# Linear attention and an ELU MLP on one core: token layout, row-tiled kv and TensorE transposes for the first batch

## Chip, cores and metric

The kernel runs on one core of a Trainium2 chip. The metric is the device time of one execution in microseconds (us); the median of several runs is given. PE is TensorE, ACT is ScalarE, DVE is VectorE, POOL is GpSimd; SP is the queue that issues DMA transposes and stores.

## What is computed

```python
def phi(x):                                   # 64 -> 128 -> 256 features
    proj = np.einsum('bhsd,df->bhsf', x, w_phi)
    proj = proj - np.max(np.abs(proj), axis=-1, keepdims=True)
    return np.concatenate([np.exp(proj), np.exp(-proj)], axis=-1)
q_p, k_p = (phi(q), phi(k))
kv = np.einsum('bhsf,bhsd->bhfd', k_p, v)
z = np.sum(k_p, axis=2)
num = np.einsum('bhsf,bhfd->bhsd', q_p, kv)
den = np.einsum('bhsf,bhf->bhs', q_p, z)[..., None] + 1e-06
attn = num / den
x = attn.transpose(0, 2, 1, 3).reshape(B * S, H * D)     # 4608 x 512
h = x @ w_in                                             # 4608 x 2048
g = np.where(h > 0.0, h, np.exp(np.minimum(h, 0.0)) - 1.0)
return g @ w_out                                         # 4608 x 512
```

There are 8 batches, 8 heads, 576 tokens, a head dimension of 64 and 128 features. All inputs and the output are float32; matmuls run in bfloat16.

## The kernel before

**Work and tiles.** Attention works on groups of four heads (a group is half a batch, 16 groups n = 0 to 15). 576 tokens are 4 x 128 + 64, so each head is loaded in two pieces: `kf`, `qf`, `vf` hold 512 tokens, four after one another in each of 128 partitions, and `km`, `qm`, `vm` hold the last 64 tokens of two heads, stacked in the two partition halves (`load_full`, `load_mixed`). The loads are issued by POOL and convert to bfloat16; a batch is nine DMAs.

**Attention.** `transposes(n)` has SP transpose k and q of a group by DMA, four DMAs. `stage_k` projects k (pieces c = 0, 1, 2; each is six matmuls of 64 rows by 128 columns, alternating between the upper and the lower half of the array: row-tiled work), takes the row maximum of the absolute value on DVE (`mk`), two exponentials on ACT (`EK`), and after the third piece the exponentials of the maxima (`em`). POOL then scales v by `em` into `vs` (line 273, all four heads at once) and the remainder into `vsm` (lines 284 and 290, two halves). `stage_qmax` does the same for q's maxima (`mq`), which are brought into rows by a DMA transpose of `mhl` into `mT`. `stage_q` projects q the other way round and subtracts the maxima by a second matmul with `sel`, then two exponentials give `Eq`. `stage_kv` multiplies `EK` with `vs` and `vsm` (40 matmuls of 128 rows by 65 columns per group; column 65 is the sum z). `stage_pn` multiplies `Eq` with `kv_sb`, divides on DVE (`xp`), and two DMA transposes put the result into `xT_sb`.

**The MLP** (named moe in the code) works on 9 chunks of 512 tokens. `moe_mm1` is four matmuls of 512 columns into `ph`, then exp on ACT into `e_sb` (line 168), min and max on POOL (line 169), and the choice on DVE into `gT` (line 172). `moe_mm2` is 16 matmuls of 512 columns into `po` for each 128 tokens, a copy on ACT and the store. A chunk is 32 items, 16 of the first kind and then 16 of the second.

**What sets the order.** The loop over n writes the pieces of a group in a list and puts MLP items from `pending` between them, 16 per group. A chunk goes into `pending` when its tokens are done, LAG pieces later. The Tile framework then orders each engine's instructions ahead of the run by its own estimate of when each is ready, and each engine runs its own queue strictly in that order. So POOL's queue holds load issues, v scaling and the MLP's e_sb in one row.

**Buffers.** PSUM is split in two pools: `pjp` with two buffers of two banks (projections, `pq`, `pn`) and `mpp` with four of one bank (`ph`, `po`, `kv`).

Of the kernel before, what the change touches and what calls it, by code (L numbers as in the profile page):

```python
# [7 lines left out]

# [8 lines left out]
def kernel(  # L17
# [20 lines left out]
    assert S == 4 * P + D and H == 8 and B % 2 == 0  # L38
# [5 lines left out]
    GH = 4  # L44
    NG = B * H // GH
    NI = 1 + GH * 2
    FULL = 4 * P
# [3 lines left out]
    N_CHUNK = NTOK // CHUNK  # L51

# [4 lines left out]
    small = ctx.enter_context(tc.tile_pool(name="small", bufs=3))  # L57
# [7 lines left out]
    w2 = consts.tile([P, F], BF16)  # L65
    for par in range(2):
        nc.gpsimd.dma_start(out=w2[par * D:(par + 1) * D, :], in_=w_phi)

    natural = {}

    def load_full(name, src, b, h0, h1):
        if (name, b) not in natural:
            natural[name, b] = (
                io.tile([P, H, 4 * D], BF16, name=name + "f"),
                io.tile([P, H // 2, D], BF16, name=name + "m"),
            )
        nc.gpsimd.dma_start(
            out=natural[name, b][0][:, h0:h1, :],
            in_=src[b, h0:h1, 0:FULL, :].rearrange("h (p s) d -> p h (s d)", s=4),
        )  # L80

    def load_mixed(name, src, b):
        pairs = src[b, :, FULL:S, :].rearrange("(pr hi) p d -> hi p pr d", hi=2)
        for hi in range(2):
            nc.gpsimd.dma_start(
                out=natural[name, b][1][hi * D:(hi + 1) * D, :, :], in_=pairs[hi]
            )

    def load(name, src, b):
        load_full(name, src, b, 0, H)  # L90
        load_mixed(name, src, b)

    for g in range(2):
        for name, src in (("k", k), ("q", q)):
            load_full(name, src, 0, g * GH, (g + 1) * GH)
            if g == 0:
                load_mixed(name, src, 0)
    load("v", v, 0)
# [3 lines left out]
    for ct in range(N_CT):  # L102
        nc.gpsimd.dma_start(out=w_in_sb[:, ct, :], in_=w_in_r[:, ct, :])
# [5 lines left out]
    for jt in range(0, N_JT, 4):  # L109
        nc.gpsimd.dma_start(  # L110
            out=w_out_sb[:, jt:jt + 4, :], in_=w_out_r[:, jt:jt + 4, :]
        )

    sel = consts.tile([P, NI, F], BF16)
    nc.vector.memset(sel, 0.0)
    for off in (0, NI, D, D + NI):
# [131 lines left out]
    def stage_k(n, c):  # L250
# [11 lines left out]
        if c < 2:  # L262
            return
# [151 lines left out]
    for c in range(3):  # L415
        stage_k(0, c)
# [84 lines left out]
```

## Time and profile before

| | us |
|---|---|
| median of 3 runs | 491.99 |
| lowest, highest | 491.56, 496.01 |
| profiled execution | 493.98 |
| span of the profiled execution (first to last instruction) | 492.0 |

The profiled execution is told by its span, in which busy times of the engines and idle times in front of instructions are given. What is busy most is not always what is waited for: a row's last part names what ended the idle time ahead of it. Matmuls are pipelined, so their durations include a latency that overlaps the next one; the pace of a row of them is the difference between two such rows of different count. The queues of the DMA engines show how many packets the loads and the transposes take:

```
q0 software_dynamic: 40896, 18.39, 31.9%
q1 hardware_dynamic: 67200, 24.14, 25.9%
```

The columns are packets, MB and the share of 16 engines' span; the first queue is POOL's loads, the second SP's transposes and stores.

### The profile page before, as it was taken

To read this page: it belongs to the slowest core of one execution; us is meant where nothing else is said; L and a number is where in the kernel's file an instruction comes from. 1 tells how busy PE (TensorE), PEld (TensorE's weight loads), DVE (VectorE), ACT (ScalarE), POOL (GpSimd) and SP (SyncE) were. 2 spreads that over 40 slices of the span, in tenths; PEclk is the share of its full clock that TensorE was granted. 3 is DMA by queue.
4 is the path that set the end of the run, shared out by engine and by line. 5 is a ranking of instruction groups with operands and counts; after the bars stand their busy time and mean duration, and the time that the engine had idled before them with its cause. 6 is when DMAs were issued, how large, how long until landed. Compare 5 with 4: busy or idle time off the path is not lost.

```text
span 492.0 us, 8615 instructions
## 1 busy us (share of the span) xinstructions
PE 374.0 (76%) x3337; PEld 189.2 (38%) x3392; DVE 238.0 (48%) x405; ACT 244.8 (50%) x405; POOL 236.3 (48%) x332
## 2 busy tenths in 40 slices
PE   0020345559699969996999699979988997999996
PEld 0010334234254425443544344434534453544442
DVE  1040154348445844684468347745754484353350
ACT  1030244367447745683569356917681768153441
POOL 8224907163916490749165825633570357052340
PEclk9999999859889999998999899989997999999999
DMA  8999996922985297429733964263231201110201
GB/s 78 141 179 177 191 149 86 129 42 49 119 123 96 47 124 117 97 50 124 115 95 56 132 124 71 50 97 93 49 60 37 70 24 24 56 57 23 64 14 71
DMA packets 108137, 43.08 MB, mean 88 GB/s; under 512 B 76352, under 2 KB 102976, under 8 KB 108096
## 3 DMA queue, kind: packets, MB, share of 16 engines
q0 software_dynamic: 40896, 18.39, 31.9%
q1 hardware_dynamic: 67200, 24.14, 25.9%
q8 instruction: 26, 0.43, 0.4%
q14 instruction: 15, 0.12, 0.1%
HBM read 36.77 MB, written 9.44 MB: 94 GB/s over the span
## 4 chain that ended last, share of the span: by engine, by line
PE 40%; POOL 18%; DMA 12%; ACT 12%; issue 9%; DVE 8%; SPq 0%; POOLq 0%; ACTq 0%
PE po L182 18%; PE ph L160 11%; POOL vs L273 6%; ACT EK L259 5%; PE kv L348 4%; DMA qf<-in_q_dram 4%; ACT Eq L336 4%; DMA vm<-in_v_dram 3%; DVE gT L172 3%; POOL e_sb L169 3%; POOL vsm L284 2%; PE pj L232 2%; ACT e_sb L168 2%; PE pn L379 2%; DMA kT<-kf 2%
## 5 line engine op out<-in xcount | busy, mean ns | idle before, releaser
L182 PE MATMUL po<-w_out_sb,gT 128*128 128x512 bf16 x547 | 143.2, 398 | 24.5 <-DVE gT L172 22.4
L160 PE MATMUL ph<-xT_sb,w_in_sb 128*128 128x512 bf16 x550 | 139.7, 386 | 9.6 <-DMA xT_sb<-xp 5.4
L169 POOL TENSOR_SCALAR e_sb<-e_sb 128x512 f32<-128x512 f32 x144 | 87.9, 614 | 95.8 <-ACT e_sb L168 90.9
L172 DVE SCALAR_TENSOR_TENSOR gT<-e_sb,ph 128x512 bf16<-128x512 f32 x144 | 95.0, 684 | 76.8 <-POOL e_sb L169 76.5
L168 ACT ACTIVATE e_sb<-ph 128x512 f32<-128x512 f32 x144 | 85.0, 606 | 47.1 <-PE ph L160 45.2
L273 POOL TENSOR_TENSOR vs<-vf,em 128x2048 bf16<-128x2048 bf16 x16 | 58.1, 3629 | 90.1 <-ACT em L266 82.8
L259 ACT ACTIVATE EK<-pj 128x768 bf16<-128x768 f32 x96 | 72.5, 811 | 49.7 <-DVE mk L242 49.4
L336 ACT ACTIVATE Eq<-pq 128x768 bf16<-128x768 f32 x96 | 72.8, 835 | 40.6 <-PE pq L328 40.6
L242 DVE TENSOR_REDUCE mq<-pj 128x6 f32<-128x768 f32 x48 | 45.8, 957 | 88.2 <-PE pj L232 88.2
L182 PEld LDWEIGHTS <-gT 128*128 128x128 bf16 x576 | 51.3, 101 | 82.0 <-DVE gT L172 26.1
L160 PEld LDWEIGHTS <-w_in_sb 128*128 128x128 bf16 x576 | 50.6, 99 | 63.8 <-issue 11.6
L191 ACT COPY o_sb<-po 128x512 f32<-128x512 f32 x36 | 21.1, 587 | 105.8 <-PE po L182 65.1
L242 DVE TENSOR_REDUCE mk<-pj 128x6 f32<-128x768 f32 x48 | 45.7, 953 | 13.5 <-PE pj L232 13.0
L232 PE MATMUL pj<-w,qT 64*128 64x128 bf16 x288 | 18.6, 241 | 43.9 <-DMA qT<-qm 28.0
L348 PE MATMUL kv<-vs,EK 128*128 128x65 bf16 x512 | 29.9, 212 | 15.9 <-POOL vs L281 12.5
L348 PEld LDWEIGHTS <-EK 128*128 128x128 bf16 x512 | 28.6, 110 | 23.9 <-issue 19.9
L232 PEld LDWEIGHTS <-qT 64*128 64x128 bf16 x288 | 11.4, 103 | 58.2 <-DMA qT<-qm 28.0
L363 DVE CAST kv_sb<-kv 128x260 bf16<-128x260 f32 x32 | 13.7, 427 | 40.8 <-PE kv L355 40.8
L379 PEld LDWEIGHTS <-Eq 128*128 128x128 bf16 x640 | 24.7, 100 | 8.2 <-DVE xp L391 2.5
L379 PE MATMUL pn<-kv_sb,Eq 128*128 128x65 bf16 x640 | 26.8, 198 | 0.0
L391 DVE TENSOR_TENSOR xp<-pn,rec 128x640 bf16<-128x640 f32 x32 | 26.3, 823 | 0.9
L355 PE MATMUL kv<-vsm,EK 128*128 128x65 bf16 x128 | 24.7, 210 | 1.2 <-POOL vsm L290 1.2
(33 smaller groups left out, 222.4 us busy)
## 6 DMA issues: line engine op xcount, KB each, us to landing
out_dram<-o_sb SPq DMA_DIRECT2D x32, 256.0 KB, 2.4
vf<-in_v_dram POOLq DMA_DIRECT2D x8, 512.0 KB, 6.5
kf<-in_k_dram POOLq DMA_DIRECT2D x7, 512.0 KB, 6.4
qf<-in_q_dram POOLq DMA_DIRECT2D x7, 512.0 KB, 8.1
w_in_sb<-in_moe_w_in_dram POOLq DMA_DIRECT2D x4, 512.0 KB, 21.5
w_out_sb<-in_moe_w_out_dram POOLq DMA_DIRECT2D x4, 512.0 KB, 12.9
xT_sb<-xp SPq DMA_TRANSPOSE x64, 2.5
out_dram<-o_sb SPq DMA_DIRECT2D x8, 128.0 KB, 2.8
```

What stands on the lines that cost most here:

```text
L160: nc.tensor.matmul(ph, w_in_sb[:, ct, jt * P:(jt + 1) * P], xT_sb[:, ct, t0:t0 + CHUNK], start=(ct == 0), stop=(ct == N_CT - 1),)
L168: nc.scalar.activation(e_sb, ph, ACT.Exp)
L169: nc.gpsimd.tensor_scalar(e_sb, e_sb, 1.0, 0.0, op0=ALU.min, op1=ALU.max)
L172: nc.vector.scalar_tensor_tensor(gT[:, jt, :], e_sb, -1.0, ph, op0=ALU.add, op1=ALU.max)
L182: nc.tensor.matmul(po, gT[:, jt, tt * P:(tt + 1) * P], w_out_sb[:, jt, :], start=(jt == 0), stop=(jt == N_JT - 1),)
L232: nc.tensor.matmul(pj[:, par, i3, :], xT[par * D:(par + 1) * D, 3 * c + i3, :], w2[par * D:(par + 1) * D, :], start=True, stop=True,)
L242: nc.vector.tensor_reduce(m[:, 3 * c:3 * c + 3, :].rearrange("p i r -> p r i"), pj, axis=AX.X, op=ALU.max, apply_absolute_value=True,)
L259: nc.scalar.activation(EK[:, sg, :, 3 * c:3 * c + 3, :], pj, ACT.Exp, scale=1.0 - 2.0 * sg)
L273: nc.gpsimd.tensor_tensor(vs[:, :, :, 0:D], vf[:, g * GH:(g + 1) * GH, :] .rearrange("p h (s d) -> p (h s) d", s=4) .unsqueeze(1).to_broad ...
L336: nc.scalar.activation(Eq[:, sg, :, 3 * c * P:3 * (c + 1) * P], pj[:, :, 0:3 * P], ACT.Exp, scale=1.0 - 2.0 * sg,)
L348: nc.tensor.matmul(kv[:, hi, sg, :], EK[:, sg, s % 2, 1 + 2 * hh + s // 2, :], vs[:, sg, 4 * hh + s, :], start=(s == 0), stop=False,)
L379: nc.tensor.matmul(pn[:, hi, t, :], Eq[:, sg, par, c0:c0 + P], kv_sb[:, hi, sg, :], start=(sg == 0), stop=(sg == 1),)
```

## The change

1. **Layout.** Tokens lie as in memory: a pair of heads is 128 partitions, each with nine consecutive tokens of 64 (`NS` = 9). The two heads of a pair are the two halves of the partitions. There is no remainder tile; `load` is one DMA for a batch (batch 0 in two halves), three per batch. `out_rows` gives for each tile two stores of 64 rows.
2. **k projection.** `w_bd` is a block-diagonal weight of 128 x 256, so a piece is three full-height matmuls of 256 columns.
3. **kv.** Contraction is over 64 partitions of one head: 72 row-tiled matmuls of 65 columns per group, alternating between the halves, into one buffer of `pjp`, and one copy for the group.
4. **v scaling.** `scale_v` runs for each pair of heads, after pieces 1 and 2 of `stage_k`; `vsm` is gone.
5. **Pieces.** `stage_q` and `stage_qmax` of the next group are one piece of the list, and so are the transposes and `stage_kv`; LAG is 3 of 9 pieces.
6. **First batch.** For the groups 0 and 1 (`PE_TRANSPOSED`) k, q, `mhl` and `xp` are transposed by TensorE with an identity matrix into `pjp` and copied by DVE; the k stage comes ahead of the q stage at the start.
7. **Set-up.** `w_phi` comes by SP's queue, the `sel` matrix is made small and widened by DVE, w_in and w_out come in two DMAs each.

```diff
+    def load(name, src, b, p0=0, p1=H // 2):
+        if (name, b) not in natural:
+            natural[name, b] = io.tile([P, H // 2, NS, D], BF16, name=name + "n")
+        nc.gpsimd.dma_start(
+            out=natural[name, b][:, p0:p1].rearrange("p r s d -> p r (s d)"),
+            in_=src[b]
+            .rearrange("h s d -> (h s d)")
+            .rearrange("(pr q x) -> q pr x", q=P, x=NS * D)[:, p0:p1],
+        )
...
+    load("k", k, 0, 0, 2)
+    ident = consts.tile([P, P], BF16)
+    make_identity(nc, ident)
+    load("q", q, 0, 0, 2)
+    load("v", v, 0, 0, 2)
+    load("k", k, 0, 2, 4)
...
+    def pe_transpose(dst, blocks):
+        tr = pjp.tile([P, 16, P], BF16, name="tr", tag="pj")
+        for j, blk in enumerate(blocks):
+            nc.tensor.transpose(tr[:, j, :], blk, ident)
+        nc.vector.tensor_copy(dst, tr[:, 0:len(blocks), :])
...
+            if n < PE_TRANSPOSED:
+                pe_transpose(dst, [nat[:, i * P:(i + 1) * P] for i in range(NI)])
+            else:
+                nc.sync.dma_start_transpose(out=dst, in_=nat)
...
+    def project_k(n, c):
+        kT = st["kT", n]
+        pj = pjp.tile([P, 8, F], FP32, name="pk", tag="pj")
+        for i3 in range(3):
+            nc.tensor.matmul(
+                pj[:, 2 * i3:2 * i3 + 2, :].rearrange("p r f -> p (r f)"),
+                kT[:, 3 * c + i3, :],
+                w_bd.rearrange("p r f -> p (r f)"),
+                start=True,
+                stop=True,
+            )
...
+        if c > 0:
+            scale_v(n, c - 1)
+
+    def scale_v(n, pr):
+        b, g = divmod(n, 2)
+        mk, em, vs = st["mk", n], st["em", n], st["vs", n]
+        r = slice(pr * NS, (pr + 1) * NS)
+        for sg in range(2):
+            nc.scalar.activation(
+                em[:, sg, r], mk[:, r], ACT.Exp, scale=2.0 * sg - 1.0
+            )
+        nc.gpsimd.tensor_tensor(
+            vs[:, :, r, 0:D],
+            natural["v", b][:, 2 * g + pr].unsqueeze(1).to_broadcast((P, 2, NS, D)),
+            em[:, :, r].unsqueeze(3).to_broadcast((P, 2, NS, D)),
+            op=ALU.mult,
+        )
+        nc.gpsimd.tensor_copy(vs[:, :, r, D], em[:, :, r])
...
-    def stage_kv(n, pr):
-        EK, vs, vsm = st["EK", n], st["vs", n], vsm_bufs[n % 2]
-        kv = mpp.tile([P, 2, 2, D + 1], FP32, name="kv", tag="mp")
+    def stage_kv(n):
+        EK, vs = st["EK", n], st["vs", n]
+        pj = pjp.tile([P, 2, 512], FP32, name="kv", tag="pj")
+        kv = pj[:, :, 0:4 * (D + 1)].rearrange("p h (r g d) -> p h r g d", r=2, g=2)
+        for pr in range(2):
             for sg in range(2):
+                for s in range(NS):
+                    for hi in range(2):
+                        rows = slice(hi * D, (hi + 1) * D)
+                        nc.tensor.matmul(
+                            kv[:, hi, pr, sg, :],
+                            EK[rows, sg, pr * NS + s, :],
+                            vs[rows, sg, pr * NS + s, :],
+                            start=(s == 0),
+                            stop=(s == NS - 1),
+                        )
...
+        if n < PE_TRANSPOSED:
+            tr = pjp.tile([P, 16, P], BF16, name="trx", tag="pj")
+            for t in range(5):
+                nc.tensor.transpose(
+                    tr[:, t, :], xp[:, t].rearrange("p h d -> p (h d)"), ident
+                )
+            nc.vector.tensor_copy(full, tr[:, 0:4, :])
+            nc.vector.tensor_copy(mixed, tr[:, 4, D:P])
...
     transposes(0)
-    transposes(1)
     for c in range(3):
-        stage_qmax(0, c)
+        stage_k(0, c)
     for c in range(3):
-        stage_k(0, c)
+        stage_qmax(0, c)
+    transposes(1)
-    LAG = 4
+    LAG = 3
...
         for c in range(3):
-            pieces.append((stage_q, n, c))
+            piece = [(stage_q, n, c)]
             if nxt:
-                pieces.append((stage_qmax, n + 1, c))
+                piece.append((stage_qmax, n + 1, c))
+            pieces.append(piece)
+        pieces.append([(transposes, n + 2), (stage_kv, n)])
...
+        if g == 0 and b > 0 and b + 1 < B:
+            load("v", v, b + 1)
         if g == 0 and b + 2 < B:
             load("k", k, b + 2)
             load("q", q, b + 2)
-        if g == 1 and b + 2 < B:
-            load("v", v, b + 2)
```

The order of POOL's queue shows two places where this moves work. The first is the start of the program. Before, from the first load on (a row with x2 or x4 is so many in a row):

```order
L67 DMA w_88<-in_w_phi_dram 64x128 x2
L77 DMA kf<-in_k_dram 128x4x256
L85 DMA km<-in_k_dram 64x4x64 x2
L77 DMA qf<-in_q_dram 128x4x256
L85 DMA qm<-in_q_dram 64x4x64 x2
L77 DMA kf<-in_k_dram 128x4x256
L77 DMA qf<-in_q_dram 128x4x256
L77 DMA vf<-in_v_dram 128x8x256
L85 DMA vm<-in_v_dram 64x4x64 x2
L103 DMA w_in_sb<-in_moe_w_in_dram 128x2048 x4
```

Now, from the first load on:

```order
L71 DMA kn<-in_k_dram 128x2x576
masks.py:197 MEMSET ident 128x128
L71 DMA qn<-in_q_dram 128x2x576
masks.py:199 ISA
masks.py:199 AFFINE_SELECT ident<-ident 128x128
L71 DMA vn<-in_v_dram 128x2x576
L71 DMA kn<-in_k_dram 128x2x576
L71 DMA qn<-in_q_dram 128x2x576
L71 DMA vn<-in_v_dram 128x2x576
L102 AFFINE_SELECT sel_small<-sel_small 128x9
L112 DMA w_in_sb<-in_moe_w_in_dram 128x2x2048
```

k of the first heads has become the first DMA of the queue, v of the first heads the third, and ahead of w_in stand six loads and the identity instead of eleven loads and w_phi.

The second place is the end of a chunk's first half in the middle of the program, where POOL's last e_sb of the chunk are waited for by DVE and then by the first po. Before:

```order
L169 TENSOR_SCALAR e_sb<-e_sb 128x512 x13
L77 DMA kf<-in_k_dram 128x8x256
L273 TENSOR_TENSOR vs<-vf,em 128x32x64
L281 CAST vs<-em 128x32
L284 TENSOR_TENSOR vsm_151<-vm,em 64x4x64
L290 CAST vsm_151<-em 64x4
L284 TENSOR_TENSOR vsm_151<-vm,em 64x4x64
L290 CAST vsm_151<-em 64x4
L77 DMA vf<-in_v_dram 128x8x256
L85 DMA vm<-in_v_dram 64x4x64 x2
L169 TENSOR_SCALAR e_sb<-e_sb 128x512 x3
```

Now:

```order
L172 TENSOR_SCALAR e_sb<-e_sb 128x512 x8
L284 TENSOR_TENSOR vs<-vn,em 128x2x9x64
L290 CAST vs<-em 128x2x9
L172 TENSOR_SCALAR e_sb<-e_sb 128x512 x5
L71 DMA kn<-in_k_dram 128x4x576
L284 TENSOR_TENSOR vs<-vn,em 128x2x9x64
L290 CAST vs<-em 128x2x9
L71 DMA vn<-in_v_dram 128x4x576
L172 TENSOR_SCALAR e_sb<-e_sb 128x512 x3
```

Between the thirteenth and the fourteenth e_sb stood ten rows' work (three of it loads' issues after the scaling, one ahead); now two loads and one half vs with its cast stand there, and the other half vs stands after the eighth e_sb.

On PE a row-tiled burst is a stretch in which all matmuls work on 64 rows of the array. Over the whole program there are 118 of them before and 73 now. In a group of the middle part each piece of k and nearly each piece of q and of its maxima was one before; now the k pieces are none, q with its maxima makes four, and kv one of 72 matmuls.

More of the change, by code (lines that the diff above doesn't have):

```diff
@@ L82, in load_mixed @@
[L82 to L97, printed above, removed]
@@ new lines @@
+    for par in range(2):
+        nc.sync.dma_start(out=w_f32[par * D:(par + 1) * D, :], in_=w_phi)
+    load("k", k, 0, 0, 2)
[4 more added lines that the diff above has]
+    load("k", k, 0, 2, 4)
+    load("q", q, 0, 2, 4)
+    load("v", v, 0, 2, 4)
+    w_bd = consts.tile([P, 2, F], BF16)
+    nc.vector.memset(w_bd, 0.0)
+    for par in range(2):
+        r = slice(par * D, (par + 1) * D)
+        nc.vector.tensor_copy(w_bd[r, par, :], w_f32[r, :])
```

295 lines of the change are left out of this document (121 added, 174 removed).

## Prediction

> **What bounds the kernel now.** I read the page first, then the busy times by stretches, then the timeline at the start and at one stall in the middle, then who waited for whom. The page gives the shape: TensorE (PE) is the engine that is busiest, and it does nothing in the first two slices.
>
> ```profile
> PE 374.0 (76%) x3337; PEld 189.2 (38%) x3392; DVE 238.0 (48%) x405; ACT 244.8 (50%) x405; POOL 236.3 (48%) x332
> PE   0020345559699969996999699979988997999996
> PEclk9999999859889999998999899989997999999999
> ```
>
> ```profile
> 0.00:28.00 28.00, 0.00 (x0) 0.00 (x0) 1.67 (x5) 1.28 (x1) 14.31 (x25) 1.00 1.15 120
> 28.00:72.00 44.00, 13.88 (x178) 9.80 (x179) 14.93 (x24) 12.09 (x18) 20.70 (x25) 1.00 1.35 176
> 72.00:120.00 48.00, 30.28 (x324) 17.90 (x328) 23.13 (x41) 24.11 (x40) 23.30 (x32) 0.82 0.63 74
> 216.00:264.00 48.00, 41.98 (x403) 20.99 (x409) 28.10 (x49) 28.80 (x49) 26.88 (x38) 0.96 0.67 98
> 450.00:492.00 42.00, 37.90 (x173) 17.11 (x175) 11.01 (x16) 14.26 (x24) 9.84 (x16) 1.00 0.14 51
> ```
>
> The first column after the stretch is its length, then come PE, PEld, DVE, ACT and POOL busy time, the granted clock, DMA share and GB/s. There are three regimes. For 28 us PE waits and only the DMA engines work. From 28 to about 94 us two groups of attention run with PE mostly idle. After that PE is the bound, at 42 of 48 us, and the granted clock of 0.96 says that something still interrupts it. The timeline of the start shows the marks that I count from:
>
> ```profile
> 6.67 1.38 SPq L218 DMA_TRANSPOSE kT<-kf  x1
> 28.03 0.82 PE L232 MATMUL pj<-w,qT 64*128 64x128 bf16 x12 [28.03 <-DMA qT<-qm]
> 48.52 3.63 POOL L273 TENSOR_TENSOR vs<-vf,em 128x2048 bf16<-128x2048 bf16 x1
> 53.62 0.60 PE L348 MATMUL kv<-vs,EK 128*128 128x65 bf16 x8 [8.52 <-POOL vs L281]
> 57.91 2.92 ACT L336 ACTIVATE Eq<-pq 128x768 bf16<-128x768 f32 x4 [20.93 <-PE pq L328]
> 94.39 1.86 PE L160 MATMUL ph<-xT_sb,w_in_sb 128*128 128x512 bf16 x4 [5.07 <-DMA xT_sb<-xp]
> ```
>
> The first MoE matmul that needs all of batch 0 runs at 94.4 us; a few that need only its early heads ran before. From there to the end are 492.0 - 94.4 = 397.6 us, and PE is the bound for nearly all of it. So the sum has two parts: where the 94.4 goes, and what happens to the 397.6.
>
> Inside the 397.6, the chain of waits and the timeline show a period of two groups, one batch, with one stall in it:
>
> ```profile
> 133.26 3.17 PE po L182 x7
> 419.13 1.25 PE po L182 x5
> ```
>
> ```profile
> 219.55 0.99 POOL L77 DMA_DIRECT2D kf<-in_k_dram  x1 [1.41 <-PE pj L232]
> 220.56 3.65 POOL L273 TENSOR_TENSOR vs<-vf,em 128x2048 bf16<-128x2048 bf16 x1
> 224.30 0.62 POOL L284 TENSOR_TENSOR vsm<-vm,em 64x256 bf16<-64x256 bf16 x1
> ...
> 225.83 0.95 POOL L77 DMA_DIRECT2D vf<-in_v_dram  x1
> 226.76 1.27 POOL L85 DMA_DIRECT2D vm<-in_v_dram  x2
> 228.11 1.77 POOL L169 TENSOR_SCALAR e_sb<-e_sb 128x512 f32<-128x512 f32 x3
> 228.76 1.88 DVE L172 SCALAR_TENSOR_TENSOR gT<-e_sb,ph 128x512 bf16<-128x512 f32 x3 [3.86 <-POOL e_sb L169]
> 229.50 2.62 PE L182 MATMUL po<-w_out_sb,gT 128*128 128x512 bf16 x7 [4.14 <-DVE gT L172]
> ```
>
> The two chain rows follow such a stall, six periods apart: (419.1 - 133.3) / 6 = 47.6 us each. In the stall PE wants the last three tiles of gT, DVE waits for POOL's e_sb, and POOL works from 219.55 to 228.11, that is 8.6 us, on v scaling and on issuing loads that stand ahead of those three in its queue. Its total is in the list of waits:
>
> ```profile
> PE po L182 <- DVE gT L172: 22.4, 8, 4.1
> PE kv L348 <- DVE gT L172: 3.4, 6, 0.6
> ```
>
> **The change part by part. The start.** Today the first projection waits until 28.0 us for a DMA transpose of qm. Afterwards TensorE transposes batch 0. The load of kf, second on POOL's queue, let its transpose go at 6.67, so a smaller first load of k can be there at about 5.5 (it is now the first on POOL's queue). The durations for what follows are these:
>
> ```profile
> L391 DVE TENSOR_TENSOR xp<-pn,rec 128x640 bf16<-128x640 f32 x32 | 26.3, 823 | 0.9
> L242 DVE TENSOR_REDUCE mq<-pj 128x6 f32<-128x768 f32 x48 | 45.8, 957 | 88.2 <-PE pj L232 88.2
> L336 ACT ACTIVATE Eq<-pq 128x768 bf16<-128x768 f32 x96 | 72.8, 835 | 40.6 <-PE pq L328 40.6
> L273 POOL TENSOR_TENSOR vs<-vf,em 128x2048 bf16<-128x2048 bf16 x16 | 58.1, 3629 | 90.1 <-ACT em L266 82.8
> ```
>
> Nine transposes of 128 columns take about 1.2 us at half clock (twice the 0.054 worked out from the ph rows below, and a latency), and the DVE copy of 1152 elements about 1.4 (0.823 for 640, scaled). So the first projection stands at about 8 us. Up to the first Eq come: three k pieces, each with one 0.96 maximum and two 0.8 exponentials behind it, the exponentials in a row (first piece 2, then 4.6); three q maxima behind them (3); the small transpose of the maxima with its copies (1); k and q of group 1, which are put ahead of it on PE and DVE (3.5 for two copies and their transposes); the first pq (0.8). That makes 15, so Eq starts at about 23 instead of 57.9. From Eq to the first full MoE matmul today are 94.4 - 57.9 = 36.5 us. Of these 5.1 are the wait for the DMA transpose of xp, which goes; in its place come four rounds of five transposes and two DVE copies, about 1.2 each, on PE and DVE, which have no other work to hide them there. I leave the 36.5. The mark goes to 23 + 36 = 59: **-35 us**. Bounds: 48 if every wait in the 36.5 shrinks as the loads come early; 75 if loads or POOL's in-order queue cost 16 us again, as the wait of 8.5 for vs does today.
>
> The loads lie under this. They are fewer and their rows longer; v of the first heads is third in the queue, so the POOL scaling that today starts at 48.5 is covered by the k and q pieces. If that cover fails, kv is late.
>
> **POOL in the steady part.** The vs of 3.6 us becomes two of about 2.1 (1152 of 2048 elements), the vsm pieces go, and nine load issues per batch become three. What stands ahead of the last three e_sb is one k load, one half vs with its cast and one v load: about 0.95 + 2.1 + 0.3 + 0.95 = 4.3 us instead of 8.6. The stall was 4.1, so 4.3 us less takes it away: **-22.4**. In return a half vs now stands in the middle of the e_sb row, where ph has four buffers ahead; its cover is 4 x 0.86 us of ph. I count 0.4 for each of 7 periods: **+3**.
>
> **Clock after the stall.** At 229.50 seven po take 2.62 us; at the cadence of the rows below they take 1.5. I take 1.1 x 7: **-8**.
>
> **Row-tiled work.** These rows show its price:
>
> ```profile
> 201.07 1.04 PE L160 MATMUL ph<-xT_sb,w_in_sb 128*128 128x512 bf16 x4
> 202.04 0.34 PE L232 MATMUL pj<-w,qT 64*128 64x128 bf16 x6
> 202.31 2.76 PE L160 MATMUL ph<-xT_sb,w_in_sb 128*128 128x512 bf16 x12
> 205.64 0.29 PE L348 MATMUL kv<-vs,EK 128*128 128x65 bf16 x4 [0.56 <-DVE gT L172]
> 205.76 0.19 PE L355 MATMUL kv<-vsm,EK 128*128 128x65 bf16 x1
> 212.87 0.80 PE L379 MATMUL pn<-kv_sb,Eq 128*128 128x65 bf16 x20
> ```
>
> Twelve ph take 2.76 and four 1.04, so one is (2.76 - 1.04) / 8 = 0.215 us, or 0.054 for 128 columns. Four ph from 201.07 end their turn at 201.93, but pj starts at 202.04; six pj are followed after 0.27, where three pairs are 0.16. So pairs on the two row halves do overlap, and each burst pays about 0.1 us on entry and again on exit. The order of PE's instructions has 118 bursts before and 73 after; 45 x 0.2 = 9, and since some fall in the start, where PE is not the bound, I count **-7**.
>
> The k projection leaves row tiling: three matmuls of 256 columns are 0.32 us where three pairs were 0.16; 3 pieces x 14 x 0.16 = **+7**.
>
> kv goes the other way, 40 full matmuls to 72 row-tiled ones. Four took 0.29 and one 0.19, so one is 0.033 and a group 1.3 us. No row shows a row-tiled matmul of 65 columns. If pairs overlap as pj's do, it is 36 x 0.033 = 1.2; if they don't, 72 x 0.033 = 2.4. I take 1.6, nearer to pj, since pairs of pj do overlap: 0.3 x 14 = **+4** (-2 to +15). The Trainium skill, TensorEngine Tiling (Array Packing), Instruction Overhead, speaks against this part: about 60 cycles for each matmul however few its columns, and no tiling where the dimension is small already. By it kv would be, as an estimate, 72 x 60 cycles at 2.4 GHz = 1.8 us a group and the sum 3 us higher; six pj of 128 columns cannot tell the two apart, as 0.16 is what either gives.
>
> kv moves from the pool of ph and po to that of the projections, so its 3.4 us of waits for gT go (**-3**). It takes a turn there instead; a group has twelve turns of some 2 us in two buffers, about 12 of its 24 us, so that hides.
>
> Sum: -35 - 22 + 3 - 8 - 7 + 7 + 4 - 3 = -61, a span of 431. The profiled run took 494.0 for a span of 492.0, and the median is 492.0; the profiled one was 2 us above the median, so I take the span as the median's equal: **431 us**.
>
> **Rivals.**
> *The stall stays.* POOL still serves loads and v scaling in one queue with e_sb, and a load may wait for transposes there. Then the -22, -8 and +3 fall out: 492 - 35 - 7 + 7 + 4 - 3 = 458. For it: the k load showed a 1.4 us wait ahead of the block. Against it: half the block is gone.
> *The start gains less.* If POOL's queue holds v scaling behind loads as in the wait of 8.5 us, the mark is at 75: 431 + 16 = 447.
> *More.* The start at 48 and kv at 1.2: 431 - 11 - 6 = 414.
> *Slower than before.* Row-tiled kv pairs don't overlap and accumulate with their latency in between, on PE in each of the 14 groups. The single matmul of 0.19 us is the worst price: 72 x 0.19 = 13.7 us a group, +12 x 14 = +170, so 600. It decides from 0.033 + 61 / (14 x 72) = 0.09 us per matmul on. Against it: pj's pairs and kv's own four in 0.29.
> *The change doesn't do what it says.* The first projection still waits for the DMA queues, the stall stays and kv costs 2.4: 492 - 7 + 7 + 15 - 3 = 504 with no start gain; it would take all three.
>
> **How the numbers follow.** Forecast 0.60; stall stays 0.14; start gains less 0.12; more 0.08; slower by kv 0.03; no effect of the start 0.03. The time is the forecast's, 431. The range from 412 to 460 takes in the case of more and both smaller gains, and leaves out the last two, the tail beyond 460 and unknown waits. About 1% is what can be told from no change. Faster by over 1% holds the first four, less a little for mixtures: 0.94; within 1% 0.03; slower 0.03.
>
> **What would show it.** The first projection at about 8 us, the first Eq at 23, the first full MoE matmul near 59; PE waits for gT ahead of po under 5 us in total instead of 22.4; granted clock near 1.0 in the middle; a period of 43 to 45 us; kv of a group at 1.2 to 1.8 us in the warm part. A first full MoE matmul after 75, a gT wait above 10, or kv above 2.4 us a group would make the prediction wrong, as would a new wait on the projections' two buffers.

## The result, and the profile after

| | us |
|---|---|
| before, median of 4 runs on the same chip | 492.96 (491.56 to 496.01) |
| changed, median of 4 runs | 430.49 (429.74 to 431.3) |
| ratio of the means | 0.8726, 95% interval 0.8678 to 0.8774 |
| span of the profiled execution (which took 431.3) | 429.5 |

The kernel became 62 us faster, and the forecast of 431 is met to 1 us. That it is so near is luck: two errors in the sum cancel, and the profile shows both. The page of the changed kernel first; its rows are busy time and share, then the span in 40 slices, then the granted clock in the same slices.

```profile
PE 370.4 (86%) x3818; PEld 195.1 (45%) x3818; DVE 241.3 (56%) x405; ACT 246.5 (57%) x437; POOL 185.2 (43%) x249
PE   2467247889998999899989998999799989899995
PEclk9999657899999999999999999999999999999999
```

PE is at work from the first slice on. The clock row has no dips any more behind the start, where before it had one every few slices; at the start it has a dip of its own, in slices 5 to 8. The busy times by stretches say how much that is (columns as in the prediction, the granted clock is the number after POOL's):

```profile
28.00:72.00 44.00, 25.37 (x332) 16.89 (x333) 19.45 (x38) 16.36 (x28) 9.93 (x10) 0.73 1.07 166
216.00:264.00 48.00, 44.73 (x484) 23.00 (x484) 31.60 (x53) 32.47 (x60) 24.16 (x33) 1.00 0.60 107
68.81:429.50 360.69, 335.55 (x3396) 170.93 (x3394) 210.38 (x348) 223.30 (x398) 159.56 (x213) 0.99 0.47 81
```

The same stretch of 48 us in the middle went from 41.98 to 44.73 us of PE and from a clock of 0.96 to 1.00. The third row is everything behind the mark from which the prediction counts. The same for the kernel before, from its mark on:

```profile
94.39:492.00 397.61, 349.86 (x3020) 172.04 (x3073) 213.12 (x361) 222.29 (x372) 189.61 (x267) 0.95 0.44 74
```

That mark, the first MLP matmul that needs all of batch 0, is the last row of the timeline of the start:

```profile
9.49 0.85 PE L251 MATMUL pk<-w_bd,kT 128*128 128x256 bf16 x3
23.03 1.51 ACT L354 ACTIVATE Eq<-pq 128x768 bf16<-128x768 f32 x2 [6.54 <-PE pq L344]
48.04 0.50 PE L300 MATMUL pm<-w_bd,qT 64*128 64x128 bf16 x6 [5.94 <-DMA qT<-qn]
55.50 0.80 POOL L71 DMA_DIRECT2D kn<-in_k_dram  x1 [13.73 <-DMA kT<-kn]
56.32 2.13 POOL L284 TENSOR_TENSOR vs<-vn,em 128x1152 bf16<-128x1152 bf16 x1
58.70 1.17 PE L372 MATMUL kv<-vs,EK 64*128 64x65 bf16 x36 [4.18 <-POOL vs L290]
68.81 0.57 PE L163 MATMUL ph<-xT_sb,w_in_sb 128*128 128x512 bf16 x1
```

The first projection at 9.5 (forecast 8) and the first Eq at 23.03 (forecast 23) are where they should be. The mark stands at 68.8, not at 59, and the rows between show where it was lost: PE waits 5.9 us for a DMA transpose of qT (group 2, the first that TensorE doesn't transpose; it was issued at 30.3 us and took 17.7), and 4.2 us in the middle of kv, whose second half of v stands on POOL behind a load of k that waited 13.7 us for the transposes of kT. Together they are 10.1 us. The k load waits for kT of group 3, which the chain of waits has with the time that it took:

```profile
40.37 14.56 DMA kT<-kn
```

The view of all operations on the tile kT says what a transpose of k takes otherwise, 3.3 us in the median:

```profile
DMA to landing us min/median/max: 3.2/3.3/14.6
```

What lay beside the slow ones is in the DMA view of the stretch from 20 to 60 us, whose digits are the busy tenths of the DMA engines in 40 slices of 1 us, and in the issues of the first 75 us (count, KB, median us from issue to landing):

```profile
DMA  9999999999999999999999699999999999950799
```

```profile
w_out_sb<-in_moe_w_out_dram POOLq DMA_DIRECT2D x2, 1024.0 KB, 31.4
```

The DMA engines are busy to nine tenths until 55 us. Loads, w_out among them, and the transposes of groups 2 and 3 share them.

From the mark to the end are 360.7 us instead of 397.6, that is 36.9 less where the prediction had 26. PE's waits behind the mark:

```profile
PE ph L163 <- DVE gT L175: 12.9, 9, 1.8
...
PE po L185 <- DVE gT L175: 0.4, 1, 0.4
```

The 22.4 us that po waited for gT are 0.4. What ph waits for gT became 12.9 from 2.9, in nine waits of at most 1.8. One of them, in the timeline of the middle:

```profile
170.94 2.12 POOL L284 TENSOR_TENSOR vs<-vn,em 128x1152 bf16<-128x1152 bf16 x1 [0.98 <-ACT em L281]
173.16 2.34 POOL L172 TENSOR_SCALAR e_sb<-e_sb 128x512 f32<-128x512 f32 x4
173.81 1.88 DVE L175 SCALAR_TENSOR_TENSOR gT<-e_sb,ph 128x512 bf16<-128x512 f32 x3 [1.90 <-POOL e_sb L172]
174.55 1.02 PE L163 MATMUL ph<-xT_sb,w_in_sb 128*128 128x512 bf16 x4 [1.51 <-DVE gT L175]
...
302.07 1.02 PE L163 MATMUL ph<-xT_sb,w_in_sb 128*128 128x512 bf16 x4 [1.52 <-DVE gT L175]
```

POOL stands idle for 1.0 us until em is there, works 2.1 us on half of v, and only then on the four e_sb that have gathered; by then all four buffers of ph are full and PE stops for 1.5 us, until the first of these e_sb has become gT. The stall has moved from the seam between ph and po into the row of ph and has become shorter: the last row is the same stall three periods later, and (302.07 - 174.55) / 3 is 42.5 us a period instead of 47.6.

The burst of kv, the term with the widest bounds, is one row:

```profile
160.41 1.33 PE L372 MATMUL kv<-vs,EK 64*128 64x65 bf16 x72
```

72 matmuls take 1.33 us with the last one's latency, at most 0.0185 us each.

### The profile page after: what moved, and what is told of

It reads as the page before. It is cut to its first block, busy times and chain, and to the rows that moved or that the text cites. A ratio compares the mean times of both kernels' runs of the same rounds, so it can differ in the third digit from the quotient of the medians.

```text
span 429.5 us, 9422 instructions
## 1 busy us (share of the span) xinstructions
PE 370.4 (86%) x3818; PEld 195.1 (45%) x3818; DVE 241.3 (56%) x405; ACT 246.5 (57%) x437; POOL 185.2 (43%) x249
## 3 DMA queue, kind: packets, MB, share of 16 engines
q1 hardware_dynamic: 59232, 22.37, 29.1%
## 4 chain that ended last, share of the span: by engine, by line
PE 51%; ACT 14%; POOL 11%; issue 11%; DVE 6%; DMA 6%; SPq 0%; POOLq 0%; ACTq 0%
PE po L185 21%; PE ph L163 14%; POOL e_sb L172 6%; ACT EK L270 5%; PE kv L372 5%; POOL vs L284 4%; DMA kT<-kn 4%; ACT e_sb L171 4%; ACT Eq L354 3%; PE pn L394 3%; PE pk L251 2%; PE pm L300 2%; DVE gT L175 2%; DVE mq L307 2%; DMA qn<-in_q_dram 1%
## 5 line engine op out<-in xcount | busy, mean ns | idle before, releaser
L163 PE MATMUL ph<-xT_sb,w_in_sb 128*128 128x512 bf16 x576 | 141.6, 385 | 14.3 <-DVE gT L175 12.9
L171 ACT ACTIVATE e_sb<-ph 128x512 f32<-128x512 f32 x144 | 82.9, 608 | 45.8 <-PE ph L163 45.5
L284 POOL TENSOR_TENSOR vs<-vn,em 128x1152 bf16<-128x1152 bf16 x32 | 67.9, 2121 | 83.4 <-ACT em L281 83.3
L270 ACT ACTIVATE EK<-pk 128x768 bf16<-128x768 f32 x96 | 72.6, 813 | 35.7 <-DVE mk L242 35.6
L307 DVE TENSOR_REDUCE mq<-pm 128x6 f32<-128x768 f32 x48 | 45.9, 957 | 49.5 <-PE pm L300 49.5
L242 DVE TENSOR_REDUCE mk<-pk 128x6 f32<-128x768 f32 x48 | 45.8, 953 | 12.4 <-PE pk L251 11.9
L251 PE MATMUL pk<-w_bd,kT 128*128 128x256 bf16 x144 | 26.3, 296 | 3.0 <-ACT EK L270 2.8
L372 PE MATMUL kv<-vs,EK 64*128 64x65 bf16 x1152 | 23.1, 198 | 5.3 <-POOL vs L290 4.2
L300 PE MATMUL pm<-w_bd,qT 64*128 64x128 bf16 x288 | 18.0, 235 | 10.9 <-DMA qT<-qn 5.9
L372 PEld LDWEIGHTS <-EK 64*128 64x128 bf16 x1152 | 20.9, 99 | 11.8 <-issue 4.3
L251 PEld LDWEIGHTS <-kT 128*128 128x128 bf16 x144 | 14.6, 105 | 15.5 <-issue 6.5
L334 PE MATMUL pq<-qT,w_bd 64*128 64x384 bf16 x96 | 17.2, 353 | 4.7 <-DVE mq L307 4.4
```

Of the source, the lines that this page charges most:

```text
L163: nc.tensor.matmul(ph, w_in_sb[:, ct, jt * P:(jt + 1) * P], xT_sb[:, ct, t0:t0 + CHUNK], start=(ct == 0), stop=(ct == N_CT - 1),)
L171: nc.scalar.activation(e_sb, ph, ACT.Exp)
L251: nc.tensor.matmul(pj[:, 2 * i3:2 * i3 + 2, :].rearrange("p r f -> p (r f)"), kT[:, 3 * c + i3, :], w_bd.rearrange("p r f -> p (r f)"), st ...
L270: nc.scalar.activation(EK[:, sg, 6 * c:6 * c + 6, :], pj, ACT.Exp, scale=1.0 - 2.0 * sg)
L284: nc.gpsimd.tensor_tensor(vs[:, :, r, 0:D], natural["v", b][:, 2 * g + pr].unsqueeze(1).to_broadcast((P, 2, NS, D)), em[:, :, r].unsqueeze ...
L307: nc.vector.tensor_reduce(mq[:, 6 * c:6 * c + 6].rearrange("p (i r) -> p r i", r=2), pj[:, :, 0:3, :], axis=AX.X, op=ALU.max, apply_absolu ...
```

## Experiments

Times are medians, ratios are of the means, to the kernel before on the same chip. That kernel's medians were 490.4 to 493.0 us on the chips used, so differences of less than 3 us between runs on different chips are not told apart. Line numbers of the experiments move by a few lines from the changed kernel's.

**1. The first batch by DMA again.**

```diff
-    PE_TRANSPOSED = 2
+    PE_TRANSPOSED = 0
```

> The changed kernel with the transposes of batch 0 given back to SP's DMA transposes; all else as changed. Theory (the start gain is made of the early projection that TensorE's transposes allow, beside loads that keep the DMA engines full): the first projection falls back from 9.5 us to 20 to 28 us, the first MoE matmul that needs all of batch 0 from 68.8 to 82 to 95 us, the part behind it stays at 361 us, and the time is 443 to 456 us. Rival (the start gain comes from the fewer and longer loads, and the transposes could have stayed with the DMA): first projection before 14 us and a time within 4 us of 430.5.

Measured: 455.09 us, ratio 0.9269 (0.9216 to 0.9323), span 453.8. Its timeline of the start:

```profile
27.78 1.46 PE L251 MATMUL pk<-w_bd,kT 128*128 128x256 bf16 x6 [27.78 <-DMA kT<-kn]
...
91.39 0.59 PE L163 MATMUL ph<-xT_sb,w_in_sb 128*128 128x512 bf16 x1 [5.38 <-DMA xT_sb<-xp]
```

The first projection waits until 27.8 us again, and the mark stands at 91.4, 22.6 later than with TensorE's transposes. Behind the mark are 453.8 - 91.4 = 362.4 us, as good as the 360.7 of the changed kernel. So the transposes are worth 24.6 us, nearly all of it in the start. Without them the other edits bring only 3 us there: 91.4 stands beside the 94.4 of before. What TensorE's transposes would bring without the other edits was not run.

**2. w_out loaded later.** The load of w_out is held back until the exponential of group 1's maxima, which POOL waits for through a write of one column.

```diff
-    for jt in range(0, N_JT, 8):
-        nc.gpsimd.dma_start(out=w_out_sb[:, jt:jt + 8, :], in_=w_out_r[:, jt:jt + 8, :])
+    def load_w_out():
+        for jt in range(0, N_JT, 8):
+            nc.gpsimd.tensor_copy(w_out_sb[:, jt, 0:1], st["em", 1][:, 0, 17:18])
+            nc.gpsimd.dma_start(out=w_out_sb[:, jt:jt + 8, :], in_=w_out_r[:, jt:jt + 8, :])
...
+        if n == 1:
+            load_w_out()
```

> The changed kernel with the load of w_out held back until POOL has scaled v of group 1 (a one-column write into w_out_sb that reads em of group 1 stands ahead of each of its two DMAs). Theory (the start came out 10 us later than forecast because DMA transposes of group 2 and 3 share the DMA engines with loads, w_out's above all; a load of k that waits for one of them then blocks POOL ahead of the v scaling): the transposes of kT land in under 8 us instead of 14.6, the wait of 4.2 us of kv for vs goes and the 5.9 us wait for qT shrinks, the first full MoE matmul stands at 58 to 63 us, and the time is 419 to 425 us. Rival 1 (the in-order chain of small steps is what bounds the start, and the waits only move): within 2 us of 430.5. Rival 2 (w_out then comes too late for the first po): a new wait of po for w_out and a time of 430 us or more.

Measured: 420.9 us, ratio 0.8566 (0.8515 to 0.8617), span 417.2. Its timeline of the start:

```profile
42.28 0.34 PE L303 MATMUL pm<-w_bd,qT 64*128 64x128 bf16 x6 [1.69 <-ACT em L284]
43.74 0.80 POOL L71 DMA_DIRECT2D kn<-in_k_dram  x1 [3.48 <-DMA kT<-kn]
...
56.89 0.38 PE L166 MATMUL ph<-xT_sb,w_in_sb 128*128 128x512 bf16 x1 [0.19 <-DVE xT_sb L426]
```

The wait for qT is gone, the load of k waits 3.5 us on POOL instead of 13.7, and the mark moves from 68.8 to 56.9, two before the 59 of the prediction. The rest, 417.2 - 56.9 = 360.3 us, doesn't change. The row of the DMA engines from 20 to 60 us shows why:

```profile
DMA  9999999999999999999929800599999998999999
```

They have room from 40 us on instead of 55, and group 3's transpose of k, issued at 38.9 us, lands after 4.3 us instead of 14.6. The expected 8 us holds for that one alone. Group 2's, beside the other loads, still take 14.4 us for k and 12.4 for q (12.6 and 17.7 in the changed kernel), and w_out, which now comes later, makes group 4's transpose of k take 15.4, for which PE doesn't wait. This kernel beats the one before and the changed one.

**3. k and q of two more groups by TensorE.** The loads stay where they are.

```diff
-            if n < PE_TRANSPOSED:
+            if n < 4:
                 pe_transpose(dst, [nat[:, i * P:(i + 1) * P] for i in range(NI)])
```

> The changed kernel, with k and q of groups 2 and 3 also transposed by TensorE; the loads stay where they are. Theory (the DMA transposes of k and q of group 2, 14.6 us long beside the load of w_out, hold PE for 5.9 us and through POOL's waiting k load hold vs, 4.2 us more): both waits go, the first MoE matmul that needs all of batch 0 comes at 59 to 62 us instead of 68.8, and the time is 420 to 425. Rival (the DMA engines are full, so that the loads of k and q of batch 1 are late themselves; PE then stands in order at its transposes for them): the mark stays at 66 or later and the time is 427 to 433.

Measured: 420.85 us, ratio 0.8611 (0.8569 to 0.8653), span 418.9. Its timeline of PE at the start:

```profile
29.13 1.17 PE L225 MATMUL tr<-ident,kn 128*128 128x128 bf16 x9
30.09 1.17 PE L225 MATMUL tr<-ident,qn 128*128 128x128 bf16 x9
...
60.28 0.38 PE L163 MATMUL ph<-xT_sb,w_in_sb 128*128 128x512 bf16 x1 [0.19 <-DVE xT_sb L423]
```

At 29.1 us kn of group 2 is there and PE transposes it without a wait, while w_out is still being loaded. So it was not the loads of k and q that were late beside w_out but their DMA transposes: whether the load goes (experiment 2) or the transposes (this one), the same 10 us come back, 8.5 of them here ahead of the mark. Both at once were not tried; in experiment 2 the waits that this edit would remove are already gone.

**4. kv without alternating halves.**

```diff
-                for s in range(NS):
-                    for hi in range(2):
+                for hi in range(2):
+                    for s in range(NS):
```

> The changed kernel with the 72 row-tiled kv matmuls of a group in another order: the nine of one half of the partitions, then the nine of the other, instead of alternating. Theory (pairs on the two halves of the array overlap; 72 take 1.33 us at full clock, 0.016 us each): without pairs each costs 0.03 to 0.036 us, so the burst takes 2.2 to 2.6 us, PE gets 14 x 1.1 = 15 us more work, and the time is 442 to 448 us. Rival (what bounds them is issue, not overlap of pairs): the burst stays below 1.5 us and the time within 3 us of 430.5.

Measured: 435.87 us, ratio 0.8881 (0.8831 to 0.893).

```profile
118.79 1.72 PE L372 MATMUL kv<-vs,EK 64*128 64x65 bf16 x72
```

The burst is 0.39 us longer than the 1.33 above, and so are the other 13 at full clock; together they make 5.5 us, and the kernel is 5.4 slower, on another chip. The time is in neither of the two expected ranges. The theory was right that alternating the halves gives overlap, but too sure that without it the halves run one behind the other, which is 72 x 0.033 = 2.4 us (0.033 being the prediction's estimate from full matmuls): with nine matmuls of one half in a row, the burst is still 0.7 us shorter than that. The starts of the single matmuls, which these rows merge, bear it out. Alternating, two of a pair start 2 to 4 ns apart and most pairs follow after 25 to 31 ns. With nine in a row, two or three starts in nine are 32 to 34 ns behind the one before, and most others 8 to 24. The two halves also write to different PSUM banks (`kv[:, hi]`), so the run doesn't separate the halves of the array from the banks.

**5. Both halves of v together**, after the third piece of k.

```diff
-        if c > 0:
-            scale_v(n, c - 1)
+        if c == 2:
+            scale_v(n, 0)
+            scale_v(n, 1)
```

> The changed kernel with both halves of a group's v scaling put behind the third piece of k, so that the first half no longer stands after the eighth e_sb of a chunk but after the ninth or tenth, and two or three e_sb stand between the halves. Theory A (ph waits 12.9 us for gT because a half vs, and POOL's wait for its em, holds POOL's queue in the middle of the first half of a chunk): the wait of ph for gT falls below 7 us, the wait of po for gT stays below 4 us, and the time is 422 to 428 us. Theory B (any placement of the scaling in that half costs the same, as ph fills its four buffers): the wait of ph stays at 11 to 15 us and the time within 2 us of 430.5. Rival C (the scaling moves back ahead of the last e_sb, and the old stall returns): po waits 10 us or more and the time is 436 to 445 us.

Measured: 438.89 us, ratio 0.8957 (0.8879 to 0.9036). Who waited on PE behind 70 us:

```profile
PE po L185 <- DVE gT L175: 11.5, 6, 4.7
PE ph L163 <- DVE gT L175: 9.0, 10, 1.8
```

Half of the old stall of po is back, at up to 4.7 us a time (4.1 before), and the kernel is 8.4 us slower with the same work in it. The third of the theories put up for it holds: what stands ahead of the last e_sb of a chunk on POOL makes the stall. In the stall at 139 us the first half stands behind the ninth e_sb of the chunk instead of the eighth, and the second behind the twelfth instead of the thirteenth. With only three e_sb between the halves, the load of k ahead of the second one also waits longer, 2.5 to 4.4 us where it was 1.4:

```profile
134.62 0.83 POOL L71 DMA_DIRECT2D kn<-in_k_dram  x1 [2.48 <-DMA kT<-kn]
```

How much of the stall is the scaling and how much the load's wait, this run doesn't tell.

**6. The kernel before, with v scaled in two halves and nothing else changed.**

```diff
+        if c > 0:
+            scale_v(n, c - 1)
+
+    def scale_v(n, hp):
...
+        h0 = g * GH + 2 * hp
+        t = slice(8 * hp, 8 * hp + 8)
...
-            vs[:, :, :, 0:D],
-            vf[:, g * GH:(g + 1) * GH, :]
+            vs[:, :, t, 0:D],
+            vf[:, h0:h0 + 2, :]
```

> The kernel before, with nothing changed but the scaling of v: heads 0 and 1 are scaled after piece 1 of k, heads 2 and 3 after piece 2, as the changed kernel does it with its halves. Theory (the block on POOL ahead of the last e_sb makes the 22.4 us that po waits for gT, and the half-clock stretches follow those stalls): the wait falls under 6, the granted clock of 216 to 264 us rises from 0.96 to 0.99 or more, and the half-clock time of the steady part, 27 us that cost about 13, goes by more than half; a wait of ph for gT of about 1.5 in each of seven periods appears (+10). 492 - 18 - 9 + 8: 468 to 478. Rival A (the nine loads, not the scaling, are the block): the po wait stays over 14 and the time is 485 to 493. Rival B (the clock drops for another reason than the stall): the wait falls but the clock stays at 0.96, 478 to 484.

Measured: 473.09 us, ratio 0.9642 (0.9584 to 0.97), span 472.5. PE's waits from its own mark (97.7) on, and then the row of that whole stretch and of the 48 us in the middle:

```profile
PE ph L160 <- DVE gT L172: 16.7, 7, 2.6
...
PE po L182 <- DVE gT L172: 2.2, 7, 0.6
```

```profile
97.69:472.50 374.81, 346.15 (x3056) 166.32 (x3055) 214.14 (x360) 224.15 (x392) 188.10 (x289) 0.97 0.50 78
216.00:264.00 48.00, 44.03 (x431) 21.12 (x430) 29.44 (x50) 31.29 (x55) 30.40 (x47) 1.00 0.89 110
```

This one edit takes 17 us off the kernel before. In the profiles the start is 3.3 us longer and the stretch behind the mark 22.8 shorter. The wait of po falls from 22.4 to 2.2, and that of ph rises from 2.9 to 16.7, which is 6.4 less in sum. PE's other waits behind the mark fall too, from 14.8 to 4.7; before, the largest of them besides kv's 3.4 for gT were these:

```profile
PE pj L232 <- ACT EK L259: 3.7, 16, 0.5
PE pj L232 <- DVE mq L242: 3.2, 1, 3.2
```

So all waits that the list has behind the mark are 40.1 us before and 23.6 now, 16.5 less. The rest is the clock: 0.95 of 397.6 us was 20 us of lost clock, 0.97 of 374.8 is 11, some 9 less. (A hundredth of clock is 4 us here, so 16.5 and 9 agree with 22.8 within the error.)

The stalls of up to 4.1 us cost clock, those of 2.4 to 2.6 us do so more rarely. Seven such stalls of ph stand here, and four of them come with a dip to half clock. One of the four, with the stretches of 3.41 us ahead of the dip and in it:

```profile
301.67 0.59 PE L160 MATMUL ph<-xT_sb,w_in_sb 128*128 128x512 bf16 x2 [2.35 <-DVE gT L172]
299.63:303.04 3.41, 1.37 (x11) 0.58 (x11) 2.11 (x4) 2.40 (x6) 3.32 (x7) 1.00 0.43 82
303.04:306.45 3.41, 3.41 (x21) 1.30 (x19) 1.28 (x2) 2.15 (x4) 3.29 (x4) 0.50 0.31 19
```

The dips in this trace begin whole multiples of 3.41 us apart. If the whole span is cut into stretches of 3.41 us that line up with them, PE was busy for 1.06 to 1.50 us in the stretch ahead of each of the four dips. The three stalls without a dip fall across the border of two stretches, and PE was busy for 1.86 us or more in each of these. So in this run the clock followed how a stall fell, not only how long it was.

**7. v in quarters**, on top of experiment 2: a pair of heads and one sign at a time, written into four different pieces of the list.

```diff
+                piece.append((mul_v, n, 1, c))
...
+            pieces[-1].append((mul_v, n + 1, 0, 0))
+            pieces.append([(stage_k, n + 1, 2), (mul_v, n + 1, 0, 1)])
```

> The kernel with the load of w_out held back (420.9 us, 12.9 us of waits of ph for gT), with v scaled in quarters of 0.9 to 1.1 us (a pair of heads, one sign), put among four different pieces, each at least a piece behind the exponential that it reads. Theory (ph waits for gT because POOL first waits 1 us for em and then works 2.1 us on a half of v ahead of four e_sb): the wait of ph falls from 12.9 under 5 and the time is 411 to 415. Rival A (the second pair of quarters now stands ahead of the last e_sb of a chunk, as in the run with v scaled together): po waits for gT 8 us or more, and the time is 419 to 428. Rival B (these waits are given back later, by ACT's or DVE's queue): 419 to 422 with the wait gone.

Measured: 425.43 us, ratio 0.8697 (0.8653 to 0.8741). The stall in the timeline:

```profile
121.60 1.15 POOL L295 TENSOR_TENSOR vs<-vn,em 128x576 bf16<-128x576 bf16 x1 [0.89 <-ACT em L284]
...
122.84 1.15 POOL L295 TENSOR_TENSOR vs<-vn,em 128x576 bf16<-128x576 bf16 x1
123.96 1.19 POOL L175 TENSOR_SCALAR e_sb<-e_sb 128x512 f32<-128x512 f32 x2
...
125.35 1.02 PE L166 MATMUL ph<-xT_sb,w_in_sb 128*128 128x512 bf16 x4 [1.56 <-DVE gT L178]
```

The framework set the two quarters behind one another again, still right after em. POOL's block is as long as that of a half, and ph waits 13.4 us in all. So this run says nothing about shorter blocks, and no expected range explains it: its time lies in that of rival A, but po waits for gT only 0.4 us. The start is 4 us later (mark at 60.98) and the rest 2 us longer, with more instructions for the same work.

**8. v scaled by DVE**, on top of experiment 2.

```diff
-        nc.gpsimd.tensor_tensor(
+        nc.vector.tensor_tensor(
             vs[:, :, r, 0:D],
```

> The kernel with the load of w_out held back (420.9 us), with the multiplication of v in halves moved from POOL to DVE; the casts of em and the loads stay on POOL. Theory (ph waits for gT, 12.9 us, because POOL waits for em and works 2.1 us on a half of v ahead of e_sb): 1152 elements take DVE about 1.5 (0.82 for 640, scaled), shorter than POOL's 2.1, and e_sb runs on beside it; the wait of ph falls under 6 and the time is 411 to 416. Rival (DVE too works in order, and the half of v with its wait for em now stands ahead of gT itself, at a price nearer to POOL's): the wait stays at 10 or more, 419 to 425.

Measured: 422.99 us, ratio 0.8581 (0.8534 to 0.8629), span 421.6. The list of PE's waits behind the start, and POOL's cast of em:

```profile
PE ph L166 <- DVE gT L178: 5.5, 8, 1.1
PE pm L303 <- DVE mq L310: 3.2, 12, 0.7
```

```profile
L293 POOL CAST vs<-em 128x18 bf16<-128x18 f32 x32 | 32.2, 1007 | 95.1 <-ACT em L284 95.1
```

The wait of ph falls from 12.9 to 5.5, as the theory has it: it does come from POOL's block. But the time stays in the rival's range, though the rival expected the wait to stay too. From the mark (62.73) to the end are 358.9 us, only 1.4 less than in experiment 2, and the start is 5.8 later, which no run explains. New waits stand on DVE's queue, of which pm for mq (3.2 us) is the largest seen; the others are not all accounted for.

**9. The k projection by row-tiled pairs**, on the changed kernel.

```diff
-            nc.tensor.matmul(
-                pj[:, 2 * i3:2 * i3 + 2, :].rearrange("p r f -> p (r f)"),
-                kT[:, 3 * c + i3, :],
-                w_bd.rearrange("p r f -> p (r f)"),
+            for par in range(2):
+                rows = slice(par * D, (par + 1) * D)
+                nc.tensor.matmul(
+                    pj[:, par, i3, :],
+                    kT[rows, 3 * c + i3, :],
+                    w_bd[rows, par, :],
```

> The changed kernel, with the k projection by row-tiled pairs again (six matmuls of 128 columns on half the rows in place of three of 256 on all), and nothing else moved. By the prediction's own terms: 3 pieces x 14 groups x 0.16 us come back (-7) and as many bursts are entered and left again at 0.2 each (+8): 428 to 433, no difference to the 430.5. Rival A (a burst costs less than 0.2, for it overlaps with the matmuls around it): 423 to 427. Rival B (the pairs don't overlap so well, or ACT and DVE take longer for the rearranged pieces): 434 to 440.

Measured: 430.65 us, ratio 0.8795 (0.8765 to 0.8826). No difference to the changed kernel that the chips would let one see (the ratio is 0.007 higher, some 3 us), as the terms of 7 and 8 us would have it. A piece of k in its timeline of PE, and one in that of the changed kernel:

```profile
141.63 0.34 PE L253 MATMUL pk<-w_bd,kT 64*128 64x128 bf16 x6
```

```profile
151.23 0.49 PE L251 MATMUL pk<-w_bd,kT 128*128 128x256 bf16 x3
```

Six in pairs take 0.15 us less than three full ones, which is the prediction's 0.16, and 42 pieces make 6 us. Since the kernels take the same time, the pairs give most of it back elsewhere. The price of going in and out of row tiling is the one candidate that the prediction had worked out from rows; that it is the cause is not shown.

## Why the prediction was right

**The sum held, its two halves did not.** The start was forecast at -35 and brought 94.4 - 68.8 = 25.6; the rest was forecast at -26 and brought 397.6 - 360.7 = 36.9. Ten too much and eleven too little. The total is right by luck; the causes it named are the ones that the runs show, but three of its sizes are off: the start's, the clock's and that of the new stall. One of its signs of being wrong, taken by the letter, came: "a gT wait above 10". It was meant for po, whose wait is 0.4, but ph waits 12.9 for gT.

**The start.** The step that failed is "I leave the 36.5": from the first Eq to the mark it took 45.8. It counted the xp transposes, but not that the first DMA transposes of k and q, those of group 2, would now fall in that stretch beside the load of w_out, and that a k load on POOL would wait for them ahead of v. The prediction named a late load in POOL's queue as a bound and as the rival "the start gains less" (75), at 0.12; 10 of its 16 us came true. Experiments 2 and 3 take the cause away in two ways, and the mark goes to 56.9 and 60.3: without that wait the forecast of 59 was good.

**The stall of po.** -22.4 forecast, -22.0 measured. Experiment 5 brings half of it back by POOL's order alone, and experiment 6 takes it out of the kernel before by cutting POOL's block in two and setting the halves apart.

**The stall's substitute.** The half of v in the row of ph was put at +3, and ph's wait is 10 longer (12.9 against 2.9). Six of its nine waits are the stall shown above, 1.5 us each. The mechanism was right and the size was not: "its cover is 4 x 0.86 us of ph" is 3.4 us, and the step forgot that POOL first waits 1.0 us for em, and that behind the block of 2.2 the first e_sb and its gT still take 1.4 (173.16 to 174.55). Together they are 4.6, which leaves 1.2 of the 1.5 uncovered. Experiment 8 shows that the block is the cause, and also that taking it off POOL in this way gains nothing.

**The clock.** -8 forecast; by the clock of the two stretches, 0.05 of 397.6 against 0.01 of 360.7, it is about -16 (a hundredth is 4 us). The step counted seven po after each stall as slow, 1.1 us each. But the dips are longer, 3.41 us or a multiple of it, and the largest, at a clock of 0.82 from 72 to 120 us, stood behind the mark and was left out. In the changed kernel that cold stretch lies almost wholly ahead of the mark, in the 0.73 of 28 to 72 us. Counted another way, PE was busy for 34.6 us at half clock behind the mark before and for 3.4 now; half of each is lost, which is 17.3 and 1.7, and again about -16. In the Trainium skill, TensorE: Matmul & The Clock Gate, Part 1, the array's clock halves after an idle window of some 3.4 us and comes back after as much work. The traces agree with the length: dips last 3.41 us or a multiple, stalls of up to 4.1 us kept the clock at 0.96 in the middle, and those of up to 1.8 us leave it at 1.00. They differ in the condition, and there the measurement decides: in experiment 6 stalls of some 2.4 us, shorter than that window, halved the clock in four of seven cases. The step lacked that a dip outlasts the seven po and that one long dip stood at the mark.

**kv.** Put at 1.6 us a group and +4, it is 1.33 and about 0, so near the lower bound, where pairs overlap. Experiment 4 shows how much of it hangs on the alternation. The 60 cycles for each matmul of the Trainium skill, TensorEngine Tiling (Array Packing), Instruction Overhead, which the prediction weighed against this part, gave 1.8 us as an estimate. The row disagrees as long as the 72 are counted one by one; for 36 pairs, one on each half, 1.33 us is 0.037 a pair, and the rule isn't violated.

**Bursts and k.** -7 and +7 were forecast; experiment 9 agrees that the k part and its bursts cancel, within the 3 us of the chips. What is left of the 36.9 when the terms above are taken out (22.0 and 16 gained, 10 lost, and the 3.4 of kv's waits for gT, which are gone) is about 5. PE's smaller waits behind the mark, 11.4 us before and 6.2 now, are as much. So the bursts, k and kv together come out near nothing, within the error of the clock; the -7 for all bursts was not tested by itself.

## What to carry to other kernels

Read an in-order queue by what stands ahead of the last item that another engine needs, not by its load: here the same work cost 8 to 17 us more or less by its place in POOL's row. A stall is to be priced with what it does to the clock behind it: in experiment 6 some 9 of the 23 us came from there. When an edit moves the start forward, look again at which transfers it now meets: a weight load that nobody needed yet cost 10 us through the transposes beside it, and moving either was enough.

## What was unexpected of the hardware

- A DMA transpose of one group took 3.3 us in the median and 14.6 where loads filled the DMA engines; nine transposes on TensorE and DVE's copy took 1.17 and 0.76 us.
- Of seven stalls of PE of 2.4 to 2.6 us, four halved the clock for 3.41 us and three didn't (experiment 6).
- Two halves of the array partly overlap even when nine matmuls of one half stand in a row (1.72 us for 72, against 1.33 alternating).
- Moving v's multiplication to DVE made POOL's little cast of em four times as long, 1.0 us in the mean. The group in experiment 2, where POOL does both one after the other, and the two side by side in experiment 8's timeline:

```profile
L293 POOL CAST vs<-em 128x18 bf16<-128x18 f32 x32 | 8.3, 261 | 0.0
```

```profile
123.52 1.36 DVE L287 TENSOR_TENSOR vs<-vn,em 128x1152 bf16<-128x1152 bf16 x1
123.55 1.45 POOL L293 CAST vs<-em 128x18 bf16<-128x18 f32 x1 [0.97 <-ACT em L284]
```

The cast ends 0.1 us after the multiplication. The Trainium skill, GPSIMD Engine Reference, Specifications, has POOL's SBUF interfaces shared with VectorE, with contention where a DVE instruction has two inputs in SBUF, as this one has. The rows agree; no run tests another cause.
